# Two-dimensional circular convolution by block transforms: the inverse transform in groups of four blocks, with frequency 0 added by row-tiled matmuls

## The chip, the cores and the metric

One core of a Trainium2 chip runs the whole program. The metric is the device time of one execution in microseconds (us). Five executions of the kernel before were timed, and one more was recorded by the hardware profiler.

## The reference

The reference convolves one image, 224 x 224 pixels of 96 channels in bf16, with a 7 x 7 filter that mixes 96 channels into 96. It does so by a two-dimensional Fourier transform, so the convolution is circular in both directions:

```python
wp = jnp.pad(w, ((0, H - K), (0, W - K), (0, 0), (0, 0)))
Xf = rfft2(x.astype(float32), axes=(1, 2))
Wf = rfft2(wp.astype(float32), axes=(0, 1))
Yf = einsum('bhwi,hwio->bhwo', Xf, Wf)
y = irfft2(Yf, s=(H, W), axes=(1, 2)).astype(bfloat16)
```

## The kernel before

The kernel transforms the rows alone (dimension H), in blocks. H is cut into 8 blocks of B = 28 rows; with the six rows of overlap a block has length 34, hence 17 frequencies (NS), two numbers (FR / NS) each: a real and an imaginary part, and for frequency 0 the two purely real ones of the block. W is convolved directly, by taps.

W is cut into seven tiles of 32 columns, counted 0 to 6 here (NT = 7, TL = 6). For each tile there are four stages:

- *Forward transform* (`a_jobs`, `f_jobs`). TensorE multiplies pixels `xn` by the matrix `Fm`; the results are copied from PSUM to `xf`. VectorE then forms sums and differences of the pixel planes, the buffers `J` (three of them, `J_bufs`; the third is used by tiles 0 and 1 alone).
- *Rounds* (`b_round`), one for each frequency s: for s above 0, 33 matmuls of 96 columns with the transformed filter `WF` into two PSUM banks, then ScalarE and VectorE combine them (`tt_`, `u`, `v`), and GpSimd or VectorE writes the sum to `yf`. After a group of rounds (`YGRP`) `yf` is written to a scratch tensor `scr` in DRAM.
- *Re-reading* (`load_t`). The scratch is read back as `tt` with blocks and frequencies on the partitions. A queue (`pend`, `pump`) lets at most NTT = 5 such buffers be held.
- *Inverse transform* (`c_jobs`). A tile has twelve jobs: two halves of 16 columns, three groups of blocks `CG` (3, 3 and 2 blocks), two jobs each. A job is two matmuls of `tt` with the matrix `G`, 384 streamed columns each, with 84 output rows for three blocks (102 rows of contraction) and 56 for two (68 rows), each into its own bank, and a copy of each bank into `yo`. After its second job the group is written to the output.

The work is laid out by hand in program order, one order for each engine. Rounds of the tile under work are the backbone. Lists of jobs for other tiles are let in after each half round (`fills`, `pace`): tile t + 1's forward transform, and inverse jobs of tiles t - 2 and t - 1, whose numbers in tile t are the two entries of `CQ[t]`. In tile 6 the sixteen jobs are four of tile 4 and twelve of tile 5. Tiles 0 and 1 run interleaved, four rounds apart.

All PSUM tiles come from one pool of eight banks (`bank`). Copies out of PSUM go to VectorE or ScalarE by a running account of their loads (`evac`). Transfers are issued by SP in program order, but for the last tile's scratch writes, which ScalarE issues (`put(SE)`).

Tile 6 has no later rounds to hide behind. Its scratch is written and read back in six parts (`prt`, `load_p`), its inverse uses two matrices, `GA` for the frequencies under 9 and `GB` for the rest; these are assembled from `G` by small transfers (`g_parts`). After the last round the first eight `GA` matmuls are done, then `WARM` matmuls with zeros into a bank that is still open, and when the last part has been read the `GB` matmuls, the copies, and eight output transfers of 168 KB follow.

Every recorded operation has line L85 of the program before (a helper issues them all), so the views tell operations apart by tiles and shapes.

Of the kernel before, what the change touches and what calls it, by code (L numbers as in the profile page):

```python
# [8 lines left out]
BF16 = mybir.dt.bfloat16  # L9
# [21 lines left out]
PGRP = ((0, 2), (2, 5), (5, 8), (8, 11), (11, 14), (14, 17))  # L31
YGRP = ((0, 3), (3, 6), (6, 9), (9, 12), (12, 15), (15, 17))
YGRPL = ((0, 3), (3, 6), (6, 9), (9, 12), (12, 15), (15, 17))
# [5 lines left out]
LAG = 4  # L39
CQ = {2: (12, 0), 3: (12, 2), 4: (10, 5), 5: (7, 8), 6: (4, 12)}  # L40
SH2 = (0, 8, 13, 17)
MERGE = ()
NP2 = 0
WARM = 38
BIAS = 3000.0
# [7 lines left out]
def kernel(  # L53
# [16 lines left out]
    C2 = C // 2  # L70
    CG = ((0, 3), (3, 3), (6, 2))
    SYNC = mybir.DependencyInfo(mybir.DependencyClass.Sync, mybir.DependencyReason.DATA)
# [65 lines left out]
    Fm = cpool.tile([R, 2, NS, JG], BF16, name="Fm")  # L138
    G = cpool.tile([3 * FR, 3 * B], BF16, name="Gm")
    KA = 4 * 2 * SA  # L140
# [135 lines left out]
    def build_g(nj):  # L276
        PG = nj * FR
# [10 lines left out]
        p = ftile([PG, 1]); sp = ftile([PG, 1]); rm = ftile([PG, 1]); jp = ftile([PG, 1]); rr = ftile([PG, 1]); z = ftile([PG, 1])  # L288
        iota(p[:], [[0, 1]], cm=1)
        mod_g(rm[:], p[:], jp[:], FR)  # L290
        mod_g(rr[:], rm[:], sp[:], 2)
        GE.tensor_single_scalar(out=z[:], in_=sp[:], scalar=0.0, op=ALU.is_equal)
        zr = ftile([PG, 1]); ag = ftile([PG, 1]); pg = ftile([PG, 1]); amp = ftile([PG, 1]); pgt = ftile([PG, 1])
        GE.tensor_tensor(out=zr[:], in0=z[:], in1=rr[:], op=ALU.mult)
        GE.tensor_scalar(out=ag[:], in0=zr[:], scalar1=17.0, scalar2=sp[:, 0:1], op0=ALU.mult, op1=ALU.add)
        GE.tensor_single_scalar(out=ag[:], in_=ag[:], scalar=2.0, op=ALU.mult)
        GE.tensor_tensor(out=pgt[:], in0=rr[:], in1=zr[:], op=ALU.subtract)
        GE.tensor_scalar(out=pg[:], in0=pgt[:], scalar1=17.0, scalar2=17.0, op0=ALU.mult, op1=ALU.add)
        GE.tensor_scalar(out=amp[:], in0=z[:], scalar1=-1.0 / L, scalar2=2.0 / L, op0=ALU.mult, op1=ALU.add)
# [3 lines left out]
        GE.tensor_scalar(out=msk[:], in0=jc[:], scalar1=jp[:, 0:1], scalar2=amp[:, 0:1], op0=ALU.is_equal, op1=ALU.mult)  # L303
        GE.tensor_scalar(out=nm[:], in0=nm[:], scalar1=ag[:, 0:1], scalar2=pg[:, 0:1], op0=ALU.mult, op1=ALU.add)
        mod_g(th[:], nm[:], fl[:], Q)

        def fin():
# [4 lines left out]
    g_fin = build_g(3)  # L312

# [154 lines left out]
    def b_round(t, s, mid, end, ydve=False, planes=()):  # L468
# [87 lines left out]
        if s == y1 - 1:  # L556
            dst, yo0 = scr_tiles[t], 0
            if t == TL:
# [12 lines left out]

    scr_tiles = {}
    tt_tiles = {}
    puts = []

    def load_t(t, gi, h):
        j0, nj = CG[gi]
        n = nj * FR
        tt = t_pool.tile([128, TW // 2, 2 * C], BF16, name="tt")
        tt_tiles[(t, gi, h)] = tt  # L580
# [20 lines left out]
    def g_parts():  # L601
        for a, b, h, r0 in prt:
            n = 2 * (b - a)
            for j in range(NJ if h else 4):
                o = GB[r0 + j * n:r0 + (j + 1) * n, j // 4] if h else GA[r0 + j * n:r0 + (j + 1) * n]
                dma(o[:, j % 4 * B:(j % 4 + 1) * B], G[2 * a:2 * b, 0:B])
                yield

    def c_jobs(t):
        jobs = []  # L610
        for h in range(2):
            for gi in range(3):
                j0, nj = CG[gi]
                hold = {}

                def mk_(q, h=h, gi=gi, j0=j0, nj=nj, hold=hold):
                    def f():
                        if q == 0:
                            hold["yo"] = yo_pool.tile([4 * B, PXC * C], BF16, name="yo")
                        tt = tt_tiles[(t, gi, h)]  # L620
                        yo = hold["yo"]
                        if True:
                            pc = psum_tile() if NP2 else None
                            for b in range(2):
                                pb = pc[:, b] if NP2 else bank()
                                TE.matmul(pb[0:nj * B, 0:4 * C], lhsT=G[0:nj * FR, 0:nj * B],
                                          rhs=tt[0:nj * FR, 4 * q + 2 * b:4 * q + 2 * b + 2, :].rearrange("p w e -> p (w e)"), start=True, stop=True)
                                if not NP2:
                                    evac(yo[0:nj * B, (2 * q + b) * 4 * C:(2 * q + b + 1) * 4 * C], pb[0:nj * B, 0:4 * C], 4 * C)
                            if NP2:  # L630
                              evac(yo[0:nj * B, q * 8 * C:(q + 1) * 8 * C].rearrange("p (b e) -> p b e", b=2), pc[0:nj * B, :, 0:4 * C], 8 * C)
                        if q == 1:
                            w0 = t * 2 * TW + h * PXC
                            dma(out[0, j0 * B:(j0 + nj) * B, w0:w0 + PXC, :].rearrange("h w c -> h (w c)"), yo[0:nj * B])
                            held[0] -= 1
                            pump()
                    return f
                for q in range(2):
                    jobs.append(mk_(q))
        return jobs  # L640
# [5 lines left out]
    def pump():  # L646
        while pend and held[0] < NTT:
            load_t(*pend.pop(0))
            held[0] += 1

    def queue_c(t):
        pend.extend((t, i % 3, i // 3) for i in range(6))
        pump()
# [24 lines left out]

    t_pool = yo_pool = None

# [21 lines left out]
    for t in range(2):  # L702
        scr_tiles[t] = dr_pool.tile([TW, NJ, NS, 4 * C], BF16, name="scr")
    bursts = {}
# [8 lines left out]
    for r in range(NS + LAG):  # L713
# [46 lines left out]
    for t in range(2, NT):  # L760
# [4 lines left out]
        else:  # L765
            scr_tiles[t] = dr_pool.tile([TW, NJ, NS, 4 * C], BF16, name="scr")
        qs = []
# [38 lines left out]
    M4 = 4 * B  # L806

    def first(g, q):
# [55 lines left out]
```

## Time and profile before

| | |
|---|---|
| times of five runs, us | 283.88, 283.89, 282.57, 283.83, 287.06 |
| median | 283.88 |
| the profiled execution's own time | 283.88 |
| its span | 282.1 |
| granted TensorE clock | 1.0 |
| transfers | 46.06 MB, mean 163 GB/s |
| tile 0 and 1 (interleaved) and what is ahead of them | 0 to 96.9 us |
| tiles 2, 3, 4, 5, 6 | from 96.9, 130.0, 162.9, 196.3, 229.9 us |
| last round's matmuls end | 262 us |

The profile is one execution, recorded by the hardware. "Busy" counts instructions on an engine; the ends of matmuls are modelled, so a busy TensorE need not be one that streams at full speed, and the distance from one matmul's start to the next says more than a matmul's length. The chain that ended last is followed back from the last instruction, at each step to what released it. In the lists a group reads: line, engine, operation, output <- inputs, shape, count, and in brackets the idle time of the engine just before and what ended it. PE is TensorE, PEld its weight loads, DVE VectorE, ACT ScalarE, POOL GpSimd, SP the engine that issues transfers.

### The profile page before, as it was taken

How to read it: one execution, taken by the hardware profiler on the slowest of the kernel's cores; microseconds unless marked ns; L12 is line 12 of the kernel's file. 1: busy time of each engine (PE TensorE's matmuls, PEld its weight loads, DVE VectorE, ACT ScalarE, POOL GpSimd, SP SyncE). 2: the span in 40 equal slices, each digit the busy share in tenths (PEclk: the TensorE clock that was granted, in tenths of full speed). 3: DMA queues.
4: the chain of work that ended last, by engine and by line, in shares of the span. 5: the costliest groups of instructions: out<-in, count | busy, mean ns of one | idle time of the engine just before them, and what ended most of it. 6: DMA issues, size and time to landing. Idle time of an engine off the chain costs nothing.

```text
span 282.1 us, 12405 instructions
## 1 busy us (share of the span) xinstructions
PE 269.3 (95%) x5240; PEld 241.7 (86%) x5240; DVE 219.7 (78%) x460; ACT 201.4 (71%) x498; POOL 97.3 (34%) x146
## 2 busy tenths in 40 slices
PE   8999999999999999999999999999999999989962
PEld 3679899999999998898989898899999898878741
DVE  5567999889789799778877886779788899857423
ACT  5459978597955658888989698987988656656023
POOL 7720214344545552242243144222422242323000
PEclk9999999999999999999999999999999999999999
DMA  6937012711111797978486876868396435877715
GB/s 178 233 93 209 5 44 61 234 45 44 46 44 73 223 227 204 260 195 271 147 222 191 237 200 167 243 184 266 97 236 194 147 106 157 231 212 199 179 47 180
DMA packets 44427, 46.06 MB, mean 163 GB/s; under 512 B 33426, under 2 KB 35454, under 8 KB 44274
## 3 DMA queue, kind: packets, MB, share of 16 engines
q1 hardware_dynamic: 43508, 43.60, 55.7%
q10 hardware_dynamic: 864, 1.67, 1.7%
q8 instruction: 41, 0.67, 1.0%
q14 instruction: 14, 0.11, 0.1%
HBM read 23.92 MB, written 21.33 MB: 160 GB/s over the span
## 4 chain that ended last, share of the span: by engine, by line
PE 65%; DVE 14%; DMA 9%; ACT 5%; issue 3%; SPq 1%; POOL 1%; DVEq 0%; ACTq 0%
PE pb L85 65%; DVE J L85 5%; DVE v L85 3%; DVE WF L85 2%; ACT WF L85 2%; DMA scrl<-yf 2%; DVE u L85 2%; DMA out_dram<-yo 2%; DMA WF<-in_x_dram 2%; DVE yf L85 2%; DMA tt<-scr 1%; SPq L85 1%; ACT xf L85 1%; DMA xf<-scrl 1%; POOL yf L85 1%
## 5 line engine op out<-in xcount | busy, mean ns | idle before, releaser
L85 PE MATMUL pb<-WF,J 96*128 96x96 bf16 x2898 | 168.0, 206 | 1.8 <-ACT yo L85 0.9
L85 PEld LDWEIGHTS <-J 96*128 96x128 bf16 x2898 | 141.0, 98 | 16.2 <-issue 9.5
L85 POOL TENSOR_TENSOR yf<-v,u 128x384 bf16<-128x384 f32 x85 | 83.8, 999 | 155.6 <-issue 106.3
L85 ACT CAST xf<-pb 96x408 bf16<-96x408 f32 (+2 forms) x146 | 67.9, 485 | 6.8 <-PE pb L85 4.9
L85 ACT CAST yo<-pb 84x384 bf16<-84x384 f32 (+1 forms) x142 | 60.3, 481 | 8.8 <-PE pb L85 7.0
L85 PE MATMUL pb<-WF,xf 96*128 96x96 bf16 x952 | 60.2, 206 | 1.3 <-DVE WF L85 0.5
L85 DVE TENSOR_TENSOR J<-xf 96x1824 bf16<-96x1824 bf16 (+1 forms) x84 | 59.1, 743 | 0.1
L85 PEld LDWEIGHTS <-xf 96*128 96x128 bf16 x952 | 47.2, 98 | 1.8 <-issue 1.2
L85 PE MATMUL pb<-Fm,xn 118*128 118x136 bf16 (+3 forms) x640 | 45.6, 199 | 0.4 <-DVE u L85 0.4
L85 PE MATMUL pb<-tt,Gm 102*84 102x384 bf16 (+1 forms) x144 | 35.9, 329 | 0.2
L85 ACT CAST WF<-pb 96x480 bf16<-96x480 f32 (+1 forms) x58 | 28.5, 568 | 5.7 <-PE pb L85 5.7
L85 PEld LDWEIGHTS <-xn 118*128 118x128 bf16 x640 | 30.5, 97 | 0.5 <-issue 0.5
L85 DVE TENSOR_TENSOR J<-J 96x912 bf16<-96x912 bf16 (+1 forms) x42 | 25.0, 595 | 0.0
L85 PE MATMUL pb<-wq 98*128 98x120 bf16 (+1 forms) x288 | 21.4, 226 | 0.0
L85 PEld LDWEIGHTS <-wq 98*128 98x128 bf16 x288 | 19.5, 150 | 0.3 <-DMA wq<-in_w_dram 0.3
L85 PE MATMUL pb<-wu 128*128 128x512 bf16 (+1 forms) x82 | 18.3, 386 | 1.0 <-DVE ct L85 1.0
L85 PEld LDWEIGHTS <-wu 128*128 128x128 bf16 (+1 forms) x82 | 9.6, 119 | 8.9 <-issue 3.1
L85 DVE TENSOR_TENSOR yf<-v,u 128x384 bf16<-128x384 f32 x27 | 15.7, 580 | 0.9
L85 PEld LDWEIGHTS <-Gm 102*84 102x84 bf16 (+1 forms) x144 | 11.4, 114 | 2.3
L85 DVE CAST WF<-pb 96x480 bf16<-96x480 f32 (+1 forms) x14 | 8.1, 612 | 6.0 <-PE pb L85 5.9
L85 ACT CAST tt<-pb 112x384 bf16<-112x384 f32 x8 | 3.6, 480 | 11.4 <-PE pb L85 11.3
L85 DVE CAST tt<-pb 112x384 bf16<-112x384 f32 x8 | 4.2, 554 | 9.2 <-PE pb L85 8.9
(391 smaller groups left out, 234.0 us busy)
## 6 DMA issues: line engine op xcount, KB each, us to landing
scr<-yf SPq DMA_DIRECT2D x30, 288.0 KB
xn<-in_x_dram SPq DMA_DIRECT2D x12, 672.0 KB
tt<-scr SPq DMA_DIRECT2D x24, 288.0 KB
out_dram<-yo SPq DMA_DIRECT2D x24, 252.0 KB
tt<-scr SPq DMA_DIRECT2D x12, 192.0 KB
out_dram<-yo SPq DMA_DIRECT2D x12, 168.0 KB
wq<-in_w_dram SPq DMA_DIRECT2D x1, 1719.0 KB
scrl<-yf ACTq DMA_DIRECT2D x5, 288.0 KB
```

What stands on the lines that cost most here:

```text
L85: r = fn(*a, **k)
```

## The change

Frequency 0 is taken out of the inverse transform's main matrix. Without it a block has 16 frequencies and 32 rows, so four blocks fill 128 rows of contraction exactly: `G` becomes 128 x 112, and eight blocks are two groups (g = 0, 1) in place of three. The two numbers of frequency 0 of all eight blocks (16 rows) are written to a scratch tensor of their own (`scrr`), read back four times into four partition ranges (`rt`: partitions 0, 32, 64 and 96 and the 15 behind each; each range holds four of the tile's 16 pairs of columns), and added by four matmuls of 16 rows with the matrix `GR`, each in its own row tile of the array (`tile_position`) and into its own bank.

A group now has six jobs, for all 32 columns (before: four jobs, two for each half). For each of two values of b: j1 does two main matmuls, j2 two more, then the four row-tiled ones, and copies the first two banks; j3 copies the last two, and for b = 1 issues the output transfer (112 rows of 6144 bytes). So a unit (g, b) holds four banks from j1, j1, j2 and j2 to the copies. Output buffers alternate between `J_bufs[2]` and one `yo`.

`CQ` gives tile 6 three jobs of tile 4 and six of tile 5; the other six of tile 5 (its group g = 1) stand behind the last round, ahead of the first `GA` matmuls, and their output goes in two transfers, one for each b. `WARM` goes from 38 to 26. `YGRP` begins with a group for frequency 0 alone, so that a tile has seven writes of scratch in place of six.

```diff
-YGRP = ((0, 3), (3, 6), (6, 9), (9, 12), (12, 15), (15, 17))
+YGRP = ((0, 1), (1, 4), (4, 7), (7, 10), (10, 13), (13, 15), (15, 17))
...
-CQ = {2: (12, 0), 3: (12, 2), 4: (10, 5), 5: (7, 8), 6: (4, 12)}
+CQ = {2: (12, 0), 3: (12, 3), 4: (9, 6), 5: (6, 9), 6: (3, 6)}
...
-WARM = 38
+WARM = 26
...
-    CG = ((0, 3), (3, 3), (6, 2))
+    M4 = 4 * B
+    FM = 2 * (NS - 1)
...
-    G = cpool.tile([3 * FR, 3 * B], BF16, name="Gm")
+    G = cpool.tile([128, M4], BF16, name="Gm")
+    GR = cpool.tile([128, 2, M4], BF16, name="Gr")
...
+        iota(mr[:], [[1, NJ], [0, B]])
+        iota(sg[:], [[0, NJ * B // 2], [1, 2]])
+        GE.tensor_single_scalar(out=r2[:], in_=rr[:], scalar=-2.0, op=ALU.mult)
+        GE.tensor_scalar(out=mr[:], in0=mr[:], scalar1=sp[:, 0:1], scalar2=1.0 / L, op0=ALU.is_equal, op1=ALU.mult)
+        GE.tensor_scalar(out=sg[:], in0=sg[:], scalar1=r2[:, 0:1], scalar2=1.0, op0=ALU.mult, op1=ALU.add)
+        GE.tensor_tensor(out=GR.rearrange("p g m -> p (g m)"), in0=mr.rearrange("p j m -> p (j m)"), in1=sg.rearrange("p m k -> p (m k)"), op=ALU.mult)
...
+    def load_t(t, g, h):
+        if g is None:
+            rt = r_pool.tile([128, TW // 4, 2 * C], BF16, name="rt")
+            tt_tiles[(t, g, h)] = rt
+            sv = scr_tiles[(t, "r")].rearrange("w j s (r e) -> (j s r) w e", r=2)
+            for i in range(4):
+                dma(rt[32 * i:32 * i + 2 * NJ], sv[:, 4 * i:4 * i + 4])
+            return
...
-        n0 = n // 16 * 16
-        for (p0, p1) in ((0, n0), (n0, n)):
-            dma(tt[p0:p1], sv[j0 * FR + p0:j0 * FR + p1, h * 8:(h + 1) * 8])
+        dma(tt[:], sv[g * 128:(g + 1) * 128, h * 8:(h + 1) * 8])
...
+    def new_yo():
+        yo_n[0] += 1
+        if yo_n[0] % 2:
+            return J_bufs[2][0:M4, 0:2 * PXC * C]
+        return yo_pool.tile([M4, 2 * PXC * C], BF16, name="yo")
...
+                def main(i, g=g, b=b, pbs=pbs):
+                    pb = bank()[0:M4, 0:4 * C]
+                    w = 4 * i + 2 * b
+                    TE.matmul(pb, lhsT=G[:], rhs=tt_tiles[(t, g, w // 8)][:, w % 8:w % 8 + 2, :].rearrange("p w e -> p (w e)"), start=True, stop=False)
+                    pbs.append(pb)
...
+                def j1(b=b, hold=hold, main=main):
+                    if b == 0:
+                        hold["yo"] = new_yo()
+                    for i in range(2):
+                        main(i)
+
+                def j2(g=g, b=b, pbs=pbs, main=main, cp=cp):
+                    for i in range(2, 4):
+                        main(i)
+                    rt = tt_tiles[(t, None, 0)]
+                    for i in range(4):
+                        TE.matmul(pbs[i], lhsT=GR[32 * i:32 * i + 2 * NJ, g], rhs=rt[32 * i:32 * i + 2 * NJ, 2 * b:2 * b + 2, :].rearrange("p w e -> p (w e)"),
+                                  start=False, stop=True, tile_position=(32 * i, 0))
+                    for i in range(2):
+                        cp(i)
+
+                def j3(g=g, b=b, hold=hold, cp=cp):
+                    for i in range(2, 4):
+                        cp(i)
...
+                    if t == TL - 1 and g == 1:
+                        sv = [v.rearrange("p (i b e) -> p i b e", b=2, e=4 * C)[:, :, b] for v in (ov, hold["yo"][0:M4])]
+                        dma(*sv)
+                    elif b:
+                        dma(ov, hold["yo"][0:M4])
...
-        pend.extend((t, i % 3, i // 3) for i in range(6))
+        pend.extend((t, *k) for k in ((0, 0), (0, 1), (None, 0), (1, 0), (1, 1)))
...
-            yo_pool = ctx.enter_context(tc.tile_pool(name="yo", bufs=3, side="right"))
+            yo_pool = ctx.enter_context(tc.tile_pool(name="yo", bufs=1, side="right"))
+            r_pool = ctx.enter_context(tc.tile_pool(name="rt", bufs=2, side="right"))
...
-    assert not cj and not pend
+    assert not pend
     load_p(4)
     load_p(5)
+    for f in cj:
+        f()
```

More of the change, by code (lines that the diff above doesn't have):

```diff
@@ L70 @@
     C2 = C // 2
-    CG = ((0, 3), (3, 3), (6, 2))
+    M4 = 4 * B
+    FM = 2 * (NS - 1)
+    assert NJ == 8 and 4 * FM == 128
     SYNC = mybir.DependencyInfo(mybir.DependencyClass.Sync, mybir.DependencyReason.DATA)
@@ L276, in build_g @@
     def build_g(nj):
-        PG = nj * FR
+        PG = nj * FM
         def floor_g(out_ap, in_ap, d):
@@ L287, in mod_g @@
             GE.tensor_tensor(out=out_ap, in0=out_ap, in1=in_ap, op=ALU.add)
-        p = ftile([PG, 1]); sp = ftile([PG, 1]); rm = ftile([PG, 1]); jp = ftile([PG, 1]); rr = ftile([PG, 1]); z = ftile([PG, 1])
+        p = ftile([PG, 1]); sp = ftile([PG, 1]); rm = ftile([PG, 1]); jp = ftile([PG, 1]); rr = ftile([PG, 1])
+        ag = ftile([PG, 1]); pg = ftile([PG, 1])
         iota(p[:], [[0, 1]], cm=1)
-        mod_g(rm[:], p[:], jp[:], FR)
+        mod_g(rm[:], p[:], jp[:], FM)
         mod_g(rr[:], rm[:], sp[:], 2)
[L292 to L299, printed above, removed]
+        GE.tensor_scalar(out=ag[:], in0=sp[:], scalar1=2.0, scalar2=2.0, op0=ALU.mult, op1=ALU.add)
+        GE.tensor_scalar(out=pg[:], in0=rr[:], scalar1=17.0, scalar2=17.0, op0=ALU.mult, op1=ALU.add)
         nm = ftile([PG, nj, B]); jc = ftile([PG, nj, B]); msk = ftile([PG, nj, B]); fl = ftile([PG, nj, B]); th = ftile([PG, nj, B])
@@ L302, in build_g @@
         iota(jc[:], [[1, nj], [0, B]])
-        GE.tensor_scalar(out=msk[:], in0=jc[:], scalar1=jp[:, 0:1], scalar2=amp[:, 0:1], op0=ALU.is_equal, op1=ALU.mult)
+        GE.tensor_scalar(out=msk[:], in0=jc[:], scalar1=jp[:, 0:1], scalar2=2.0 / L, op0=ALU.is_equal, op1=ALU.mult)
         GE.tensor_scalar(out=nm[:], in0=nm[:], scalar1=ag[:, 0:1], scalar2=pg[:, 0:1], op0=ALU.mult, op1=ALU.add)
         mod_g(th[:], nm[:], fl[:], Q)
+        r2 = ftile([PG, 1]); mr = ftile([PG, NJ, B]); sg = ftile([PG, NJ * B // 2, 2])
+        iota(mr[:], [[1, NJ], [0, B]])
[4 more added lines that the diff above has]
+        GE.tensor_tensor(out=GR.rearrange("p g m -> p (g m)"), in0=mr.rearrange("p j m -> p (j m)"), in1=sg.rearrange("p m k -> p (m k)"), op=ALU.mult)
         def fin():
@@ L310, in build_g @@
         return fin
-    g_fin = build_g(3)
+    g_fin = build_g(4)
     def prep_jobs(gi):
@@ L556, in b_round @@
         if s == y1 - 1:
-            dst, yo0 = scr_tiles[t], 0
-            if t == TL:
+            if t < TL:
+                dst, yo0 = (scr_tiles[t], 1) if s else (scr_tiles[(t, "r")], 0)
+            else:
                 i = sum(s >= b for b in PARTS[1:])
@@ L572, with new_scr @@
     scr_tiles = {}
+    def new_scr(t):
+        scr_tiles[t] = dr_pool.tile([TW, NJ, NS - 1, 4 * C], BF16, name="scr")
+        scr_tiles[(t, "r")] = dr_pool.tile([TW, NJ, 1, 4 * C], BF16, name="scrr")
     tt_tiles = {}
     puts = []
-    def load_t(t, gi, h):
-        j0, nj = CG[gi]
-        n = nj * FR
+    def load_t(t, g, h):
[6 more added lines that the diff above has]
+            return
         tt = t_pool.tile([128, TW // 2, 2 * C], BF16, name="tt")
-        tt_tiles[(t, gi, h)] = tt
+        tt_tiles[(t, g, h)] = tt
         sv = scr_tiles[t].rearrange("w j s (r e) -> (j s r) w e", r=2)
-        n0 = n // 16 * 16
-        for (p0, p1) in ((0, n0), (n0, n)):
-            dma(tt[p0:p1], sv[j0 * FR + p0:j0 * FR + p1, h * 8:(h + 1) * 8])
+        dma(tt[:], sv[g * 128:(g + 1) * 128, h * 8:(h + 1) * 8])
     TW2 = 2 * TW * C
@@ L604, in g_parts @@
             for j in range(NJ if h else 4):
-                o = GB[r0 + j * n:r0 + (j + 1) * n, j // 4] if h else GA[r0 + j * n:r0 + (j + 1) * n]
-                dma(o[:, j % 4 * B:(j % 4 + 1) * B], G[2 * a:2 * b, 0:B])
-                yield
+                o, c0 = (GB[:, j // 4] if h else GA[:]), j % 4 * B
+                r = r0 + j * n
+                if a == 0:
+                    dma(o[r:r + 2, c0:c0 + B], GR[0:2, 0, 0:B])
+                    dma(o[r + 2:r + n, c0:c0 + B], G[0:n - 2, 0:B])
+                else:
+                    dma(o[r:r + n, c0:c0 + B], G[2 * a - 2:2 * b - 2, 0:B])
@@ L609, in c_jobs @@
+                yield
+    yo_n = [0]
+    def new_yo():
[3 more added lines that the diff above has]
+        return yo_pool.tile([M4, 2 * PXC * C], BF16, name="yo")
     def c_jobs(t):
         jobs = []
[L611 to L639, printed above, removed]
@@ new lines, in c_jobs, with cp @@
+        for g in range(2):
+            hold = {}
+            for b in range(2):
+                pbs = []
+                def main(i, g=g, b=b, pbs=pbs):
[3 more added lines that the diff above has]
+                    pbs.append(pb)
+                def cp(i, b=b, pbs=pbs, hold=hold):
+                    o = (2 * i + b) * 4 * C
+                    evac(hold["yo"][0:M4, o:o + 4 * C], pbs[i], 4 * C)
+                def j1(b=b, hold=hold, main=main):
[15 more added lines that the diff above has]
+                        cp(i)
+                    w0 = t * 2 * TW
+                    ov = out[0, g * M4:(g + 1) * M4, w0:w0 + 2 * PXC, :].rearrange("h w c -> h (w c)")
+                    if t == TL - 1 and g == 1:
[3 more added lines that the diff above has]
+                        dma(ov, hold["yo"][0:M4])
+                    if b:
+                        held[0] -= 2
+                        pump()
+                jobs.extend((j1, j2, j3))
@@ L646, in pump @@
     def pump():
-        while pend and held[0] < NTT:
+        while pend and (pend[0][1] is None or held[0] < NTT):
+            held[0] += pend[0][1] is not None
             load_t(*pend.pop(0))
-            held[0] += 1
     def queue_c(t):
-        pend.extend((t, i % 3, i // 3) for i in range(6))
+        pend.extend((t, *k) for k in ((0, 0), (0, 1), (None, 0), (1, 0), (1, 1)))
         pump()
@@ L677 @@
     load["v"], load["a"] = BIAS, 0.0
-    t_pool = yo_pool = None
+    t_pool = r_pool = yo_pool = None
     def pace(q, k):
@@ L702 @@
     for t in range(2):
-        scr_tiles[t] = dr_pool.tile([TW, NJ, NS, 4 * C], BF16, name="scr")
+        new_scr(t)
     bursts = {}
@@ L765 @@
         else:
-            scr_tiles[t] = dr_pool.tile([TW, NJ, NS, 4 * C], BF16, name="scr")
+            new_scr(t)
         qs = []
@@ L805 @@
         pools["psb"] = ctx.enter_context(tc.tile_pool(name="pst", bufs=8, space=bass.MemoryType.PSUM))
-    M4 = 4 * B
     def first(g, q):
```

## The prediction

> **What bounds the kernel now.** I read the page's shares first, then the chain that ended last in order of time, then the busy time by stretch with one stretch per tile, then the groups by form and the timeline inside one stretch.
>
> ```profile
> PE 269.3 (95%) x5240; PEld 241.7 (86%) x5240; DVE 219.7 (78%) x460; ACT 201.4 (71%) x498; POOL 97.3 (34%) x146
> ```
>
> ```profile
> 162.94 58.27 PE pb L85 x1128
> ...
> 264.33 5.56 DMA scrl<-yf
> ...
> 269.95 2.70 DMA xf<-scrl
> ...
> 272.78 1.49 PE pb L85 x7
> ```
>
> The chain runs on TensorE almost without a break while tiles 2 to 5 are worked on: what goes in or out of TensorE's queue there goes straight into the time. From 264.33 on it is another regime: one write, one read back, and a short burst, with TensorE idle or warming.
>
> ```profile
> 196.30:229.90 33.60, 33.41 (x649) 30.15 (x647) 27.72 (x60) 27.67 (x71) 10.83 (x11) 1.00 0.57 164
> 229.90:262.00 32.10, 31.02 (x583) 26.90 (x583) 25.33 (x54) 18.71 (x49) 10.80 (x11) 1.00 0.67 185
> ```
>
> These are tile 5 (index from 0) and tile 6 (columns: TensorE, weight loads, VectorE, ScalarE, GpSimd, clock, DMA). TensorE is 33.4 of 33.6 us in the first; the last tile leaves it 1.1 us idle.
>
> ```profile
> 180.60 0.28 PE L85 MATMUL pb<-Fm,xn 118*128 118x136 bf16 x2
> 180.72 0.49 PE L85 MATMUL pb<-tt,Gm 102*84 102x384 bf16 x2
> 181.04 0.33 PE L85 MATMUL pb<-WF,J 96*128 96x96 bf16 x4
> ...
> 182.57 0.34 PE L85 MATMUL pb<-Fm,xn 118*128 118x136 bf16 x3
> 182.84 0.51 PE L85 MATMUL pb<-tt,Gm 68*56 68x384 bf16 x2
> 183.29 0.34 PE L85 MATMUL pb<-WF,J 96*128 96x96 bf16 x4
> 184.10 0.34 PE L85 MATMUL pb<-Fm,xn 118*128 118x136 bf16 x3
> 184.28 0.76 PE L85 MATMUL pb<-WF,J 96*128 96x96 bf16 x14
> ```
>
> Ends of matmuls are modelled, so I read starts. A pair of three-block matmuls (84 columns) holds TensorE from 180.72 to 181.04, 0.33 us. Three Fm matmuls take 0.18 (184.10 to 184.28), so the two-block pair (56 columns) was due at 182.75; the round goes on at 183.29: 0.54 us for the same 768 streamed columns. The extra 0.21 lies about half ahead of the pair (182.75 to 182.84) and half in and behind it. In the built program only the 56-column matmuls have another array tile, 128x64 in place of 128x128, so I read 0.21 as the price of going into another tile mode and back.
>
> **The change, part by part.** *Removed:* 144 inverse matmuls, 48 pairs at 0.33 and 24 pairs at 0.54: 15.8 + 13.0 = 28.8 us of TensorE time, all inside the bound stretches.
>
> *Added:* 24 units (six tiles, two row groups, two halves), each of four 112-column main matmuls and one set of four 16-row matmuls in 32x128 tiles. A main costs 0.162 (38 warming matmuls of this shape: 6.34 less the last one's 0.33, over 37), so 0.65 for four. No row shows row tiles beside each other. A set's upper bound is one after the other, 0.21 + 4 x 0.162 = 0.86; its lower bound is one streaming time plus three of the shortest steps between starts (0.026: from 7.92 us on, 96 Fm matmuls on the first pixels take 2.69, less the last one's 0.19, over 95), 0.21 + 0.162 + 0.08 = 0.45. The four use different row groups and different banks, so nothing in the program orders them; I take 0.45.
>
> The Trainium skill ("TensorE: Matmul & The Clock Gate", Part 3, Measured speedup vs the span model) gives four row tiles at 512 columns a speedup of 3.07; from that page I estimate 0.21 + 0.65/3.07 = 0.42 for a set and 0.7 us less in all.
>
> Two of the 24 units go behind the last round (next paragraph). 22 x (0.65 + 0.45) = 24.2, against 28.8: **-4.6 us**; with the serial end 22 x 1.51 = 33.2: +4.4.
>
> *Behind the last round.* Two units, 2.2 us, stand where TensorE now warms until 270.2 and then waits for the last read-back at 272.78; twelve fewer warming matmuls (1.9) make room. Their eight copies run on VectorE and ScalarE after the last sum (264.3) at four each, some 2 us, while both sit idle until 273.16. If that cover were gone they would cost 2.2 plus 2. Their two output transfers, 688 KB, are queued on SP behind the last read-back (269.95) and ahead of the eight final outputs (first at 273.83). From 275 to 278 the DMA moves 266 GB/s, so 688 KB need 2.6 us after about 1 us of start, done near 274.2, in a gap that is now empty (27 GB/s from 272 to 275). Bounds 0 to 0.9; I take **+0.2**.
>
> *Last tile.* Sixteen jobs there (10 x 0.33 + 6 x 0.54 = 6.5) become three units (3.3); that is in the -4.6. Today it also stalls:
>
> ```profile
> 251.11 0.33 PE L85 MATMUL pb<-WF,J 96*128 96x96 bf16 x4 [0.60 <-ACT yo L85]
> ...
> 253.59 0.85 ACT L85 CAST yo<-pb 84x384 bf16<-84x384 f32 x2 [1.08 <-DMA out_dram<-yo]
> ...
> 254.12 0.33 PE L85 MATMUL pb<-WF,J 96*128 96x96 bf16 x4 [0.31 <-ACT yo L85]
> ```
>
> Copies wait for an output buffer still being written out, and TensorE for their banks: 0.60, then 0.31, and between them a two-block pair of 0.78 that took 0.51 above: 1.2. With two larger buffers, each filled once in that tile, this should go: **-1.2**, bounds 0 and -1.2.
>
> *The new wait.* Each unit's first two banks are filled in job j1 and copied only behind the set in j2; two rounds' and some Fm banks are taken between. All eight banks of the pool can then be in use. In the built order three sets (one in tile 4, two in tile 5) are followed directly by a round whose first matmul needs the very bank that the first copy behind that set empties, and their second main needs the bank of the Fm copy just ahead. Price: a 384-column matmul's start to its copy's start is 0.38 (272.78 in the chain to 273.16 below), the copy 0.48, TensorE again 0.06 later: 0.92, of which the rest of the set and the way out (0.08 + 0.162 + 0.1) cover 0.34, so some 0.59; the stall above was 0.60. The second main: some 0.45 by the same steps. 3 x 1.04 = 3.1, and half a us for one set in tile 2 whose mains wait for VectorE's sums: **+3.6**. Queued behind the waiting matmul is the whole round, then VectorE's and ScalarE's work on it. Lower bound 0 (copies run ahead); upper bound 15 sets x 0.59 = 8.9, since in 15 of 22 sets four other banks are taken in between and the next matmul wants the ninth.
>
> ```profile
> 273.16 4.47 DVE L85 CAST tt<-pb 112x384 bf16<-112x384 f32 x8 [8.87 <-PE pb L85]
> ```
>
> The Trainium skill ("TensorEngine Tiling (Array Packing)", PSUM Bottleneck) speaks against the change: tiling speeds TensorE up but not the emptying of PSUM, which may then bind. By that rule the upper bound would be the likely one and the time 287.5.
>
> *At no cost.* 48 fewer copies (about 23 us, nearly all ScalarE) shorten nothing, as ScalarE is busy 27.7 of 33.6. The frequency-0 matrix adds GpSimd work before its 4.9 us wait for ScalarE's sine at 16 to 21 us, and the first sum on it is at 34.25: hidden, at most 2 us if that wait were gone. SP issues fewer transfers, so what stands behind them (pixel loads) is not later; one put more per tile goes out at its first round. Tile 5's first load is 384 KB in place of 288; today it is issued at 235.82 and wanted at 239.94, where TensorE waits 0.1: +0 to 0.8, I take **+0.3**.
>
> Sum: -4.6 + 0.2 - 1.2 + 3.6 + 0.3 = -1.7. The profiled execution took 283.88 (span 282.10 and 1.78 around it), which is also the median of the five runs: **282.2 us**.
>
> **The rivals.** *Free banks* (0.15): copies run ahead because ScalarE has lost 23 us, and the +3.6 is gone: 278.6. For it: ScalarE has 6 us idle per tile. Against: the copy cannot start before the set. *Banks bind everywhere* (0.14), the other side: the next round waits at all 15 sets, 8.9 in place of 3.6, giving 287.5. It decides for slower once more than about 12 sets wait 0.59, for 4.6 + 1.2 - 0.5 + 1.4 = 6.7 must be eaten. *Tiles in series* (0.10): the packing does not do what it says, a set costs 0.86, +9.0 on my sum: 291.2. Nothing in the trace excludes it. *VectorE binds the last tile* (0.03): TensorE's need falls to 32.1 - 3.2 - 1.2 = 27.7 beside VectorE's 25.3; if its order costs 1.2, 283.4.
>
> **How the numbers follow.** My forecast (0.58) has its own range 280.4 to 284.6: from the three round waits alone (1.8 of the 3.6) to half as much waiting again (+1.8) with the last tile's stalls half kept (+0.6). Half a per cent, 1.4 us, is about what a measurement of this kernel can tell from no change. Of my 0.58, 0.32 lies under 282.5, 0.23 within, 0.03 above; free banks add 0.15 to faster; banks everywhere 0.01 to no change and 0.13 to slower; series 0.10 to slower; VectorE 0.03 to no change: 0.47, 0.27, 0.26. The range takes in free banks and most of the waiting case, and leaves out the series: 278.4 to 287.0.
>
> **What would show it.** Right: starts of the four 16-row matmuls some 0.03 apart and the round on 0.45 after the set's first due time; no 56-column form; three waits of the round on a copy of yo or J2, tiles 4 and 5 not shorter, the last tile nearer 28 us; the stretch from the last sum to the end still 17.8. Wrong: starts 0.16 apart; waits of about 0.6 behind most sets; a step in or out of the row tiles far from 0.1; final outputs that start later than 9.5 us after the last write's issue.

## The result and the profile after

The changed kernel takes 0.9949 of the time of the kernel before, with an interval of 0.9933 to 0.9965. The medians are 282.76 us against 285.28 us, and 0.9949 of 285.28 is 1.45 us less. Here and below a ratio compares the fast runs of both kernels, while a time in us is the median of all runs, slow ones too (all 50 runs against all 92 would give 0.991). A second comparison, made later on another set of runs, gave 0.9942 (0.9903 to 0.998). So the change is a gain of half a per cent: at the very bound of what can be told from no change, and close to the 1.7 us of the sum. The sum's terms are another matter.

The profiled execution took 282.54 us, its span 280.8. First the chain that ended last, in order of time (start, length, what):

```profile
178.86 25.10 PE pb L87 x509
...
206.50 5.78 PE pb L87 x117
...
213.92 24.22 PE pb L87 x495
...
242.82 4.71 DMA rt<-scrr
...
267.48 8.33 PE pb L87 x49
```

Before, one row of 58 us covered tile 4 and most of tile 5. Now that run of TensorE is cut three times, at 178.86, 206.50 and 213.92, and each cut is a round that starts late. At 242.82 stands a transfer that the prediction did not have on the path: the read-back of the frequency-0 rows. Then busy time by stretch, for tile 5, tile 6 and all that is behind the last round:

```profile
199.47:234.49 35.02, 33.43 (x659) 30.03 (x657) 26.40 (x57) 25.14 (x65) 10.76 (x11) 1.00 0.55 159
234.49:263.11 28.62, 27.59 (x577) 25.26 (x575) 25.88 (x56) 12.03 (x31) 10.82 (x11) 1.00 0.71 188
263.11:280.83 17.72, 12.55 (x79) 8.61 (x76) 8.20 (x17) 5.67 (x13) 0.00 (x0) 0.93 0.65 190
```

Tile 5 is longer than before (33.59 us from start to start): 1.6 us of it is TensorE idle, against 0.2 before. Tile 6 is 3.3 us shorter. By place, with "behind the last round" counted from the start of the last round's final matmul:

| place | forecast, us | first profiles | second profile of the changed kernel against the first before |
|---|---|---|---|
| start of the rounds | 0 | 20.80 to 23.48: +2.7 | 23.85: +3.1 |
| tiles 2 to 5 | +2.2 (56 jobs 22.3 out, 19 units 20.9 in, waits 3.6) | 133.01 to 134.87: +1.9 | 134.90: +1.9 |
| tile 6 | -4.1 (6.5 out, 3.3 in, stalls -1.2, first load +0.3) | 31.92 to 28.63: -3.3 | 29.42: -2.5 |
| behind the last round | +0.2 | 20.32 to 17.71: -2.6 | 18.44: -1.9 |

The two middle rows add up to -1.4 and -0.6; the timed runs show -1.45. The outer two are large and nearly cancel in the first pair, and the experiments had to say whether they belong to the program.

A set of four row-tiled matmuls, in the timeline:

```profile
184.24 0.52 PE L87 MATMUL pb<-tt,Gm 128*112 128x384 bf16 x2
184.69 0.38 PE L87 MATMUL pb<-rt,Gr 16*112 16x384 bf16 x4
185.00 0.34 PE L87 MATMUL pb<-WF,J 96*128 96x96 bf16 x4
```

From the second main's start to the first 16-row start is 0.254 us: 0.162 of streaming and 0.092 for the way in. The four starts are 0.003 apart, and 0.297 after the last one the round goes on: 0.162 and 0.135 for the way out. A set costs 0.092 + 0.010 + 0.297 = 0.40 us. At 177 the same step looks like this:

```profile
177.19 0.32 PE L87 MATMUL pb<-tt,Gm 128*112 128x384 bf16 x1
177.68 0.32 PE L87 MATMUL pb<-tt,Gm 128*112 128x384 bf16 x1 [0.17 <-ACT xf L87]
177.93 0.38 PE L87 MATMUL pb<-rt,Gr 16*112 16x384 bf16 x4
178.33 0.86 ACT L87 CAST yo<-pb 112x384 bf16<-112x384 f32 x2 [0.70 <-PE pb L87]
178.86 0.33 PE L87 MATMUL pb<-WF,J 96*128 96x96 bf16 x4 [0.56 <-ACT yo L87]
```

The second main comes 0.49 after the first instead of 0.16, waiting for the copy of the Fm bank, and the round comes 0.92 after the set instead of 0.30, waiting for the first `yo` copy. The first step is 0.33 late and the second 0.62. The same picture stands at 206.50 and 213.92.

### The profile page after: what moved, and what is told of

Read it like the earlier page. It is cut to its first block, busy times and chain, and to the rows that moved or that the text cites. A ratio compares the mean times of both kernels' runs of the same rounds, so it can differ in the third digit from the quotient of the medians.

```text
span 280.8 us, 12302 instructions
## 1 busy us (share of the span) xinstructions
PE 267.2 (95%) x5276; PEld 240.4 (86%) x5276; DVE 219.8 (78%) x461; ACT 185.2 (66%) x449; POOL 101.4 (36%) x147
## 4 chain that ended last, share of the span: by engine, by line
PE 48%; DVE 7%; issue 3%; ACT 2%; DMA 2%; POOL 1%; SPq 1%; DVEq 0%; ACTq 0%
PE pb L87 48%; DVE J L87 3%; DMA rt<-scrr 2%; DVE v L87 2%; DVE yf L87 1%; ACT yo L87 1%; DVE u L87 1%; POOL yf L87 1%; ACT xf L87 1%; SPq L87 1%; DVE tt L87 0%; DVEq L902 0%; ACT tt__6846 L87 0%; ACT tt__7197 L87 0%; ACT tt__3032 L87 0%
## 5 line engine op out<-in xcount | busy, mean ns | idle before, releaser
L87 PE MATMUL pb<-WF,J 96*128 96x96 bf16 x2898 | 164.7, 206 | 2.5 <-ACT yo L87 1.7
L87 PEld LDWEIGHTS <-J 96*128 96x128 bf16 x2898 | 138.9, 98 | 10.0 <-issue 6.7
L87 ACT CAST WF<-pb 96x480 bf16<-96x480 f32 (+1 forms) x58 | 28.6, 568 | 8.0 <-PE pb L87 7.8
L87 PE MATMUL pb<-tt,Gm 128*112 128x384 bf16 x96 | 24.2, 327 | 0.9 <-ACT xf L87 0.6
L87 PE MATMUL pb<-wq 98*128 98x120 bf16 (+1 forms) x288 | 22.2, 233 | 1.6 <-DMA wq<-in_w_dram 1.6
L87 ACT CAST J<-pb 112x384 bf16<-112x384 f32 x48 | 20.6, 483 | 4.7 <-PE pb L87 2.7
L87 ACT CAST yo<-pb 112x384 bf16<-112x384 f32 x44 | 18.8, 483 | 6.3 <-PE pb L87 6.3
L87 PE MATMUL pb<-wu 128*128 128x512 bf16 (+1 forms) x70 | 16.3, 394 | 1.1 <-DVE ct L87 1.1
L87 PEld LDWEIGHTS <-wu 128*128 128x128 bf16 (+1 forms) x70 | 8.0, 117 | 8.2 <-issue 2.7
L87 PEld LDWEIGHTS <-Gr 16*112 16x112 bf16 x96 | 3.4, 121 | 9.7 <-issue 9.7
L87 ACT COPY xf<-xf 96x816 bf16<-96x816 bf16 (+3 forms) x20 | 11.2, 617 | 0.0
```

Source lines behind the costliest of these rows:

```text
L87: r = fn(*a, **k)
```

## The experiments

All ratios are to the kernel before, run beside it on the same chip. `k0` and `km` below count half rounds.

**1. Inverse jobs let in later (the waits for banks).** On the changed kernel:

```diff
-        k0 = 10 if t == 2 else 3
+        k0 = 10 if t == 2 else 6
```

> The changed kernel, but in tiles 3 to 6 the inverse jobs start at half round 6 instead of 3 (k0); nothing is added or left out. Theory (bank waits): in the changed kernel's trace three sets, in tiles 4 and 5, are followed by 0.76 us of TensorE waiting for a copy of its own first bank, with 0.33 to 0.47 just ahead of it: 3.4 us. In the later order no round's first matmul takes the bank of a unit that is still held, so tiles 4 and 5 shrink by about 1.1 and 2.3 us and the time is some 3.5 us under the changed kernel's, ratio to the kernel before about 0.982. Rival (the waits only show where the copies' engine is late anyway): moving the jobs moves the waits, tiles 4 and 5 stay within 0.5 us, ratio 0.995.

Measured: 0.9815 (0.9754 to 0.9875), 279.81 us. The three long waits are gone (one of 0.19 beyond the usual way out remains, at 205.41). Tiles 4 and 5 went from 33.9 and 35.0 to 33.3 and 33.0 us, tile 3 from 33.4 to 32.7. In the profile tile 6 came out longer, but its row names the reason:

```profile
196.71:229.66 32.95, 32.83 (x659) 29.95 (x656) 27.11 (x59) 25.00 (x65) 10.88 (x11) 1.00 0.58 168
229.66:261.51 31.85, 30.84 (x577) 28.22 (x575) 25.57 (x54) 11.84 (x31) 10.80 (x11) 0.89 0.65 169
```

The column after GpSimd's is the granted clock: 0.89 in tile 6. That stretch can't be compared with one at 1.00. Tile 5 can, and there the theory of the waits holds: the same instructions in another place among the rounds, 2.1 us less.

**2. Tile 6's jobs spread further (the frequency-0 rows).** On the changed kernel, the half round of tile 6 from which the jobs of tile 5 are let in:

```diff
-            km = 11
+            km = 14
```

> The changed kernel, but in tile 6 the first job of tile 5 starts at half round 14 instead of 11 (km). Theory: the second set of tile 6 waits 1.2 us (0.25 + 0.96) for the frequency-0 rows that are read in four transfers behind two tt loads; three half rounds (2.5 us) later they have landed, the wait is gone and the stretch of tile 6 falls from 28.6 to about 27.4 us; ratio to before 0.991. Rival (the wait is covered, as VectorE sets tile 6): the wait goes, the stretch stays at 28.6, ratio 0.995.

Measured: 0.9851 (0.9804 to 0.9898), 280.65 us. What it takes away is this, in the changed kernel's timeline:

```profile
246.04 0.73 PE L87 MATMUL pb<-rt,Gr 16*112 16x384 bf16 x2
247.57 0.53 PE L87 MATMUL pb<-rt,Gr 16*112 16x384 bf16 x2 [0.80 <-DMA rt<-scrr]
```

The four 16-row matmuls of one set, elsewhere 0.003 apart, start at 246.04, 246.45, 247.57 and 247.79, as the four parts of `rt` come in one after another. The round behind them starts 1.7 us later than behind an ordinary set. SP issues the four transfers from 241.29 on, behind two of `tt`, and the one of 242.82 takes 4.71 us to land (in the chain above). With the set later nothing waits for them. Tile 6 is 27.62 us in place of 28.63, at a clock of 1.00 in both. The ratio fell by more, 2.8 us, and beyond the range that was expected. Of that, 0.9 us is the kernel before, whose runs behind this ratio average 284.9 us against 283.9 in the first comparison. Another 0.6 may be the clock: the runs of this kernel have a mean granted clock of 0.998, those of the changed kernel 0.995, and among the latter 0.01 of clock goes with some 2 us (an estimate from its runs).

**3. The deferral undone.** All twelve jobs of tile 5 in tile 6, with the 38 warming matmuls of before:

```diff
-CQ = {2: (12, 0), 3: (12, 3), 4: (9, 6), 5: (6, 9), 6: (3, 6)}
+CQ = {2: (12, 0), 3: (12, 3), 4: (9, 6), 5: (6, 9), 6: (3, 12)}
-WARM = 26
+WARM = 38
```

> The changed kernel with the second half of tile 5 inside tile 6 again (CQ[6] = (3, 12)) and 38 warming matmuls: the move behind the last round is undone. Forecast's sum: two units, 2.2 us of TensorE, come back into tile 6 and 0.2 us of transfers leave the end: +2.0 us, ratio 1.002. Theory from the changed trace: the move also freed the last scratch write, whose way from issue to the GB matmuls fell from 8.45 to 6.64 us, since no output transfer is issued just ahead of it: then +2.2 and +1.8, ratio 1.009. Rival (that write's time varies from run to run): the way stays near 6.6 us and the ratio is 1.002.

Measured: 1.0043 (1.0005 to 1.0082), 286.03 us. The deferral is worth 0.9% inside the changed kernel, 2.7 us: the interval takes in the rival's 1.002 and leaves out the theory's 1.009, and from the last write's issue to GB it is 6.8 us, as the rival had it. The stretch behind the last round did not go back to 20.3: it is 17.9, so the deferral had not made it shorter.

**4. The four matmuls in one row tile.**

```diff
-TE.matmul(pbs[i], lhsT=GR[32 * i:32 * i + 2 * NJ, g], rhs=rt[32 * i:32 * i + 2 * NJ, 2 * b:2 * b + 2, :]..., tile_position=(32 * i, 0))
+TE.matmul(pbs[i], lhsT=GR[0:2 * NJ, g], rhs=rt[0:2 * NJ, 2 * b:2 * b + 2, :]..., tile_position=(0, 0))
```

All four take the first partition range of `rt`, so three of four pairs of columns get another pair's frequency 0.

> The changed kernel with all four 16-row matmuls of a set in the same row tile (position 0, reading the first range of rows): it leaves out frequency 0's right values for three of four banks. Theory (the row tiles run beside each other, starts 3 ns apart in the changed trace): here starts are 0.16 apart, each set costs 3 x 0.16 = 0.48 more, 22 sets 10.5 us in the rounds, less where a set is followed by a bank wait; ratio to before 1.03. Rival (the starts in the trace are only those of queueing and the array works them off one by one): the round behind a set starts no later than now, ratio 0.995.

Measured: 1.0187 (1.013 to 1.0245), 289.86 us.

```profile
182.79 0.32 PE L87 MATMUL pb<-tt,Gm 128*112 128x384 bf16 x1 [0.17 <-ACT xf L87]
183.05 0.85 PE L87 MATMUL pb<-rt,Gr 16*112 16x384 bf16 x4
183.83 0.34 PE L87 MATMUL pb<-WF,J 96*128 96x96 bf16 x4
```

The starts are 0.207 and then 0.162 apart now, and from the first of them to the round it is 0.78 in place of 0.31: what the rival "tiles in series" of the prediction would have looked like. Running beside each other is worth 2.4% of the kernel; without it the change would have been slower. The price is rather more than that, as this kernel reads only the first part of `rt` and does not wait for the others: tiles 2 to 5 took 144.1 us in place of 134.9, tile 6 28.0 in place of 28.6.

**5. Edits 1 and 2 together.**

> Both single edits on the changed kernel together: the inverse jobs let in from round 6 on (in place of 3) in tiles 3 to 6, and in tile 6 the fill list closed by round 14 (in place of 11). Theory (the two edits take away different stalls: the first the waits for banks in tiles 4 and 5, 3.4 us; the second the waits for the frequency-0 rows in tile 6, which the first had made larger): about 5 us less than the changed kernel, tiles 4 and 5 at 33.3 and 33.0 us as with the first alone, tile 6 back from 31.85 to 28 to 29, ratio to the kernel before 0.972 to 0.980. Rival (they share one saving: what the first moves out of tiles 4 and 5 is paid in tile 6 whatever its order, which the second cannot cure): tile 6 stays at 31 us or more, ratio 0.981 to 0.985.

Measured: 0.9739 (0.9651 to 0.9828), 276.53 us. Tiles 4, 5 and 6 take 32.6, 33.0 and 27.2 us at a full clock: TensorE waits 0.5 us in the three of them. The two edits take away different waits, and the rival (one saving, shared) is out.

**6. The deferral alone, on the kernel before.**

```diff
-CQ = {2: (12, 0), 3: (12, 2), 4: (10, 5), 5: (7, 8), 6: (4, 12)}
+CQ = {2: (12, 0), 3: (12, 2), 4: (10, 5), 5: (7, 8), 6: (4, 6)}
-WARM = 38
+WARM = 26
...
     load_p(5)
+    for f in cj:
+        f()
```

> The kernel before, three-block and two-block groups and all, with one part of the change alone: the last six inverse jobs of tile 5 (one half of its columns) stand behind the last round, and 26 warming matmuls in place of 38. Theory (moving work out of the last tile is worth its TensorE time plus the stalls on output buffers there, and the end has a gap to take it): tile 6 from 31.9 to 28.5 to 29.5 us, the end unchanged, at 20.3 or at the 17.7 to 18.4 of the other kernels if the 20.3 was chance, ratio 0.986 to 0.992. Rival 1 (the end grows by the moved work, as its three transfers or its copies are on the path): the end 1.5 us or more above that of the unedited kernel in this call, ratio 0.993 to 1.0. Rival 2 (the moved work is what makes the end shorter): unedited 20.3, this one under 18.5, ratio under 0.985.

Measured: 1.0126 (1.0065 to 1.0188), 287.84 us: slower, beyond even the first rival. Tile 6 fell to 27.9 us, further than expected, but the stretch behind the last round grew to 25.9. In the timeline of that stretch, and its row by windows:

```profile
264.24 1.75 ACT L85 CAST yo<-pb 84x384 bf16<-84x384 f32 x4 [1.71 <-DMA out_dram<-yo]
...
267.62 2.78 PE L85 MATMUL pb<-xf,GA 72*112 72x384 bf16 x8 [4.56 <-DMA xf<-scrl]
270.19 6.00 PE L85 MATMUL pb<-wu 128*112 128x384 bf16 x26
276.02 0.98 PE L85 MATMUL pb<-xf,GB 128*112 128x384 bf16 x5
```

```profile
258.96:284.88 25.92, 15.36 (x75) 10.22 (x72) 9.20 (x19) 6.59 (x15) 0.00 (x0) 0.78 0.68 169
```

The deferred copies wait for an output buffer still being written out. The first GA matmul waits 4.56 us, until 267.62, put down to the read-back; the copies had ended by 266.3. The chain of this profile agrees: it goes from the last scratch write (261.23, 3.37 us) to read-backs that SP issues from 264.61 on, and from them to GA. So the copies' wait is seen, but that it is what holds the end is not shown. And TensorE, idle until then, comes back at a low clock: the 26 warming matmuls start 0.32 apart for the first ten steps, where they take 0.16 at full clock, and they stand in front of GB. The same deferral that gains 2.7 us with the change costs 3.6 us without it.

**7. No set.** The changed kernel without the row-tiled matmuls:

```diff
-                    for i in range(4):
-                        TE.matmul(pbs[i], lhsT=GR[32 * i:32 * i + 2 * NJ, g], ...)
```

> The changed kernel without the row-tiled matmuls: frequency 0 is still written, read back and its matrix built, but not added. Theory (a set costs TensorE 0.40 us in 22 places of the rounds, and with the sets gone the waits for banks keep their places but begin earlier): 22 x 0.40 = 8.8 us less in the rounds, and the waits for the frequency-0 rows (1.2) gone too; ratio 0.957 to 0.965. Rival (the copies out of the banks are what binds, so time without the sets turns into waits for banks): tiles 3 to 5 fall by under 0.8 us each in place of 1.6, ratio 0.972 to 0.985.

Measured: 0.9761 (0.9695 to 0.9827), 277.79 us. The total is the rival's, the rounds are the theory's: tiles 2 to 5 fell by 6.6 us, 0.35 for each of 19 sets where a set costs 0.40. Tile 6, with three sets and the wait for `rt` out, fell by only 0.2, and behind the last round it took 19.4 us in place of 17.7, but at a clock of 0.88, which can't be compared. In tile 6 TensorE was busy 26.2 of 28.4 us. Of the other 2.2 it waited 0.86 for a sum of VectorE's (until 231.62) and 1.14 for the transfer of tile 5's first `tt` (until 237.13).

**8. The kernel before, profiled again.**

> The kernel before, unedited, profiled a second time, for its two ends. If the start of the rounds at 20.8 us and the end of 20.3 us in its first profile belong to the program, both come again within 0.5 us; then the change costs 1 to 2.7 us at the start and gains 2 to 2.6 at the end. If they are chance, the rounds start at 21.9 to 23.5 and the end takes 17.7 to 18.4, as in the five profiles of the changed kernel and its variants, and neither may be put down to the change.

Measured: the rounds started at 22.16, not 20.80, and the stretch behind the last round took 17.54 us, not 20.32. Of the 2.8 us between the two, 1.8 are one transfer: from the issue of the last scratch write to the issue of the read that waits for it, 5.6 us the first time and 3.8 the second. This profile too has a disturbed tile 6:

```profile
231.48:265.00 33.52, 32.33 (x581) 28.27 (x581) 26.04 (x55) 19.20 (x50) 10.81 (x11) 0.95 0.67 183
```

33.52 us at a clock of 0.95, against 31.92 at 1.00. So the 2.6 us gained behind the last round in the first pair of profiles can't be put down to the change.

**9. The changed kernel again.**

> The changed kernel, unedited, for a second profile and for a comparison with the kernel before in the same call as the three kernels beside it. In the first profiles the stretch from tile 2 to the end took 181.2 us with the change and 185.3 and 184.3 without, 3.1 to 4.0 less, while the timed runs gave 0.9949, 1.5 us less. Theory (the shares from tile 2 on are the program's, and the rounds start later by chance, as they start anywhere from 20.8 to 23.5 us in these profiles): tile 2 to the end again 181 to 182, ratio 0.987 to 0.993. Rival (the change costs about a us and a half ahead of the rounds, by its work on the new matrix): ratio 0.993 to 0.997, and the rounds start above 22.2 us in this profile too.

Measured: 0.9942 (0.9903 to 0.998), 283.03 us. Tile 2 to the end took 182.8 us, above the theory's 182, and the rounds started at 23.85, as the rival had it. But the rival named work that all the kernels built on the changed one do as well, and nine of them (experiments 1 to 5, 7 and 10 to 12) start their rounds at 21.2 to 22.5 us, 22.0 in the mean; the kernel before started at 20.8 and 22.2. The timelines show what sets the start. In twelve of the fourteen profiles the rounds begin 4.5 us after the first matmul on the filter `wq`, and that one starts at 16.3 to 18.0 us, in all but the first profile of before after waiting for the transfer of `wq`. In the two profiles of the changed kernel it starts at 17.9 and 18.4, and the way from it takes 5.5 us: the granted clock from 0 to the first round is 0.93 in these two, and 1.00 in the twelve others. So one of the three us is the clock of these two executions, the rest the landing of a transfer that every kernel has. Nothing supports a cost of three us at the start; one of under a us can't be excluded, and stays open.

**10. One output buffer.**

```diff
-        if yo_n[0] % 2:
+        if False:
             return J_bufs[2][0:M4, 0:2 * PXC * C]
```

> The changed kernel with one output buffer in place of two that alternate: every group of an inverse waits until the group before has been written out. Theory (the second buffer is what lets the deferred jobs run behind the last round without a wait, which the three small buffers of the kernel before did not): tiles 2 to 5 within 0.7 us each, as a group's output has half a tile's time to leave; tile 6 at 28.6 to 30 us; the end from 17.7 to 20 or more, as the copies behind the last round wait for the output of the group before; ratio to the kernel before 1.000 to 1.015. Rival (outputs leave in time anyhow, and the long end of the kernel before with deferral had another cause): tile 6 and the end within 0.5 us of the changed kernel's, ratio within 0.003 of its.

Measured: 1.0152 (1.0083 to 1.0222), 291.34 us, six us over the changed kernel. The clock was 0.91 in tile 4 and 0.85 in tile 6 of its profile, so only tile 3 is compared by length, and the waits by name (from the waits: who waited, for what, us in total, times, longest):

```profile
131.34:166.28 34.94, 33.76 (x658) 30.09 (x656) 26.55 (x58) 23.62 (x61) 10.76 (x11) 1.00 0.73 206
```

```profile
ACT yo L87 <- DMA out_dram<-yo: 13.9, 6, 6.6
```

Tile 3 took 33.4 with two buffers. ScalarE waits up to 6.6 us for an output to leave; the changed kernel has no such wait. That half a tile's time would be enough for it was wrong. The buffer costs time throughout, not behind the last round alone.

**11. Fewer warming matmuls.**

```diff
-WARM = 26
+WARM = 18
```

> The changed kernel with 18 warming matmuls in place of 26. In its profile the last read-back is issued at 268.08 and the warming ends at 272.03, where the GB matmuls follow without a pause; the kernel before's second profile has 2.8 us from that issue to the first GB matmul. Theory (the warming itself now holds the end): the first GB matmul comes 2.7 to 2.9 us after the issue of the last read-back, in place of 3.95, and the time falls by 1.0 to 1.3 us: ratio to the changed kernel 0.9955 to 0.9965. Rival (the read-back lands no earlier than the warming ends, or the clock falls in the gap): no gain, or up to 1 us more.

Measured: 0.9934 (0.9896 to 0.9973), 281.93 us; the unedited kernel beside it has 0.9942. The difference is inside the intervals: no gain shown. In the profile GB came 2.78 us after the issue of the last read-back, as expected, but the next experiment shows that this is not dependable.

**12. Edits 1, 2 and 11 together.**

> The changed kernel with three edits: inverse jobs from round 6 on, tile 6's fill list closed by round 14, 18 warming matmuls. The first two gave 0.9739 (interval 0.9651 to 0.9828) with tiles 2 to the end at 176.3 us. Theory (the third is independent, as it acts behind the last round alone): tile 2 to the end at 175.0 to 175.5 us, ratio to the kernel before 0.965 to 0.975. Rival: no less than 176, ratio 0.974 or more.

Measured: 0.9729 (0.9668 to 0.979), 276.29 us: the shortest of the kernels here, and not told apart from experiment 5.

```profile
195.95:228.90 32.95, 32.83 (x658) 29.95 (x656) 27.10 (x59) 25.00 (x65) 10.87 (x11) 1.00 0.61 177
228.90:256.11 27.21, 26.85 (x577) 25.02 (x575) 25.12 (x54) 11.86 (x31) 10.78 (x11) 1.00 0.70 198
```

```profile
265.47 0.99 PE L87 MATMUL pb<-xf,GB 128*112 128x384 bf16 x5 [1.64 <-DMA xf<-scrl]
```

Tiles 5 and 6 are the same as in experiment 5. Behind the last round the warming ended early, and TensorE waited 1.64 us for the read-back, which took 3.96 us from its issue to GB. Tile 2 to the end took 176.3 us, as the rival had it; the ratio lies in the theory's range, and its interval in both.

## Why the prediction came out as it did

*The units (-4.6).* A set was put at 0.45 and measures 0.40. The error lies in the steps between starts: 0.026 each was the shortest in the trace of before, and row tiles start 0.003 apart. The way in and out, 0.227, was 0.02 dearer than the 0.21. The estimate from the Trainium skill ("TensorE: Matmul & The Clock Gate", Part 3) was 0.42, and lies nearer. At 0.40 the 22 units are 23.1 us and the term -5.7. Experiment 4 shows that the set really overlaps, experiment 7 that 0.35 of the 0.40 is on the path in tiles 2 to 5.

*The new wait (+3.6).* Right in place and nearly in size: the three sets named wait, one in tile 4 and two in tile 5, and none in tiles 2 and 3. By starts, each round is 0.62 late (forecast 0.59) and each second main 0.33, 0.47 and 0.33 (forecast 0.45): 3.0 us, and 0.6 at the set whose mains wait for VectorE's sums, where 0.5 was put (it is the first of tile 3, at 137.5 to 138.0, not one of tile 2). Smaller waits stand in no term: with sets at 0.40 the row of tiles 2 to 5 would be +1.3, and +1.9 was measured. Experiment 1 takes the long waits away by moving the jobs three half rounds. The rule of the Trainium skill ("TensorEngine Tiling (Array Packing)", PSUM Bottleneck) binds the next round at three sets of 22 in the order as built, not everywhere, so the rival at 287.5 is out. "Free banks" at 278.6 did not happen, but the changed order brings it about: 0.9815 of 283.88 is 278.6.

*The last tile (-3.2, -1.2).* The stalls on the output buffers are gone as forecast. Experiments 10 and 6 say more than the term did: without the second large buffer the same kernel is 2.1% slower, and in the kernel before, with its three small ones, the deferral does not pay; that the buffers are why is argued, not shown.

*Tile 5's first load (+0.3, bounds 0 to 0.8).* This is the step that failed. It priced a larger `tt` load, and overlooked that the four `rt` transfers go out on SP behind it and that a set needs all four. The round behind one set is 1.7 us late, in both profiles, twice the bound. With 1.7 in place of 0.3 the tile's sum is -2.7, between the -3.3 and -2.5 of the two profiles. Experiment 2 removes the wait, and the tile is 1.0 us shorter. The `tt` load alone, which the term did price, is waited for 0, 0.4 and 1.1 us (the two profiles and experiment 7), once above the bound as well.

*Behind the last round (+0.2).* 17.71 and 18.44 us, against 20.32 in the first profile of before and 17.54 in the second: the profiles allow anything from a gain of 2.6 to a loss of 0.9, and the term can't be settled by them. The step took the first profile's end for the program's own. What is on this path is two transfers and the warming, and each part varies by more than the term: in thirteen profiles (all but experiment 6) it takes 2.4 to 5.6 us from the write's issue to that of the read that waits for it, and 2.8 to 5.3 from there to GB, which in six of them follows the warming without a wait.

*The sum.* -1.7 against -1.45 was luck in part: the set too dear (1.1) was cancelled by the frequency-0 rows too cheap (0.7 by experiment 2, 1.4 by the starts) and the smaller waits (0.6). The bound of 0.5% falls inside the interval of the result, so faster and no change can't be told apart by more than a hair, as the chances of 0.47 and 0.27 had it. The serial rival's price, 291.2, is close to what experiment 4 gives: 1.0187 of 283.88 is 289.2. VectorE, the last rival's engine, is busy 25.9 of 28.6 us in tile 6 and 25.1 of 27.2 in experiments 5 and 12; of the 1.0 us that TensorE is idle in tile 6, 0.8 is a wait for `rt` and 0.2 one for VectorE.

## What to carry to other kernels

When a step takes more banks for longer, the saving and the new wait are of the same size: count which matmul needs the bank next, and move the step among its neighbours before judging it, as a shift by three half rounds made a gain of 0.5% one of 1.9%, and with the second edit 2.6%. A part of a change can turn its sign without the rest (the deferral: 2.7 us won in the changed kernel, 3.6 lost in the kernel before), and so parts are priced together with what they stand on. A step that needs several transfers waits for the last of them: all are counted, in the order in which they are issued. A stretch of one profile is compared only at the same granted clock, and a stretch that hangs on one or two transfers only over several profiles.

## What the runs showed of the hardware

Four 16-row matmuls in four row tiles start 0.003 us apart at 384 columns; in one row tile they start 0.207 and then 0.162 apart (experiment 4). Going from whole-array matmuls into the row tiles costs 0.092 us, coming back 0.135.

The granted clock of one core falls for stretches of single executions, to 0.89 and 0.95 over tile 6 in the rows above; in the kernel before the tile was 1.6 us longer for it (33.52 against 31.92). In experiments 1, 3, 8 and 11 such a stretch of tile 6 runs at half clock for 3.4 us (6.8 in experiment 1) and begins 1.1 to 2.4 us after the start of a pause of TensorE of 0.7 to 1.4 us; behind pauses of 0.8 and 0.9 us there, in the two profiles of the changed kernel, none begins. In experiment 6 TensorE stood idle for 4.56 us, until 267.62, and resumed at half speed: the eight GA matmuls and the first ten warming steps start 0.32 apart, the later ones 0.16. The granted clock is 0.50 from 263.2 to 273.4 us, so it had fallen when the pause had hardly begun. In both profiles of the changed kernel it was 0.93 ahead of the first round.
